# Banks of PSUM for the later bias units and for the small products, in a kernel of attention with a learned distance bias and a gated layer

## The chip, the cores and the metric

The kernel runs on one core of a Trainium2 chip. The metric is the time of one execution on the device, in microseconds (us), as the median of the runs; lower is better.

## The reference

Four sequences of 576 positions with 8 heads of width 64 go through attention with an additive bias, and the result, 2304 tokens of width 512, through a gated layer of width 1536:

```
rel  = pos[:, None] - pos[None, :]
x    = log1p(|rel|) / log1p(max(pos[:, None], 1))
bias = relu(x * w1 + b1) @ w2                    # (576, 576, 8 heads), hidden width 32
attn = softmax(q @ k.T / 8 + bias)               # per sequence and head
x    = (attn @ v), heads side by side            # 2304 x 512
out  = ((x @ w_a) * (x @ w_b)) @ w_out           # 512 -> 1536 -> 512
```

All inputs and the output are 32-bit floats; the large weights reach the kernel as 64-bit floats.

## The kernel before, in words

**Attention.** Two heads (a pair) of one sequence are a unit. The first half of the schedule takes query positions 0 to 255 of all units, the second half the other 320. A unit is cut into tiles of 128 queries against all 576 keys, 144 tiles in all. One tile is a chain over the engines: TensorE makes the scores in a pair of PSUM banks (`qk`, L444, or L458 for the first units), VectorE adds the bias row block and takes the minimum (L472), ScalarE takes the exponential (L477), GpSimd and VectorE form the reciprocal sum (L505, L506), GpSimd multiplies (L508), TensorE transposes (`tp`, L521), ScalarE and VectorE copy out (L526; L538 to L540), and after the last tile of a unit (of a pair of tiles, for the first four units) TensorE multiplies by the values (`pv`, L555, or L488). ScalarE and VectorE copy that out into the layer's input `x` (L495 and L496; L567 and L569). `attn_steps` issues this as two steps per tile, with loads some tiles ahead.

**The layer.** A block of 256 tokens takes 12 chunks `f` of the width 1536; for each, 12 products of `x` with w_a and then 12 with w_b go into one PSUM bank (`ab`, L649), ScalarE and VectorE copy out and multiply (L657, L659, which gives `g`), and after the chunks two outputs `o` of 36 products each follow (L698). Of the tag `ab`, which `o` shares, there are three banks.

**Weights.** `wab_steps` and `wo_steps` turn the 64-bit weights into 32-bit ones (`wt`, ScalarE L244, VectorE L245 to L249, from the load `wraw`, L238) and split them. A scale that is a power of two is found per pair of chunks by two small products: `pow2_down` (L62) transposes a column of maxima so that VectorE can reduce it (L66 to L72), and `pow2_up` (L75) spreads the result over the partitions (L77, L79). The same two serve the scale of the values of each sequence (`v_scale`). There are 10 of each in the program. Both put their product, `pr`, into the one PSUM bank of `pv`.

**The bias.** It depends on the positions alone and is made once, in 36 units of 16 query positions for all heads (`bias_unit`, L138): four hidden groups `h` (VectorE L126 or ScalarE L130), four products of each into PSUM (`psta`, L136), two scaled copies by ScalarE (`bo`, L151 and L154: one for each direction of the distance), and a store to DRAM, from where tiles load their rows (L424). Units over 512 columns are cut in two at column 288. The first 16 units come before attention. The 20 later ones (`bias_stream`, L806) are spread over tiles of the second and third sequence: `attn_steps` makes one, at times two, after the scores of a tile were read and before the next scores are issued. Their `psta` takes the pair of banks of the scores.

**PSUM.** Of the 8 banks `qk` has two, `tp` two, `pv` one, and the pools `eq` (two banks, at first) and `mps` (the three of `ab`, later) share the other three, of which one is unused while `eq` is open.

**Order.** TensorE's order is the program's own, fixed by `merge`, which interleaves the generators by their step counts. The other engines' queues are ordered by a scheduler when the kernel is built. Every engine's queue runs in order, as does that of SyncE (SP), which issues the loads.

```
ps = pvp.tile([128, 512], F32, tag="pv", name="pr")             # L63, L76
ab = mps.tile([128, 2, TOK], F32, tag="ab", name="ab", bufs=3)   # L644
pss = banks()                                                    # L145, one pair for both cuts
bg, lambda: qkp.tile([128, 2, 512], F32, tag="qk", name="psta", bufs=1), u, un, int(un % 4 != 3), 1, 2   # L809
```

Of the kernel before, what the change touches and what calls it, by code (L numbers as in the profile page):

```python
# [7 lines left out]
F32 = mybir.dt.float32  # L8
# [17 lines left out]
TOK = 256  # L26
# [21 lines left out]
def attention_moe(ctx, tc, q0d, q1d, kd, vd, idn, wp, wa, wb, wo, lsw, lg, rl, out):  # L48
    nc = tc.nc
    PSUM = bass.MemoryType.PSUM  # L50
# [8 lines left out]
    xt, cpool, epool, xpool = [], [None], [None], [None]  # L59
    vsc = []  # L60

    def pow2_down(mx, n, tag):  # L62
        ps = pvp.tile([128, 512], F32, tag="pv", name="pr")  # L63
        nc.tensor.matmul(ps[0:n, 0:128], mx, tab["idn"], start=True, stop=True)
        m = att.tile([n, 1], F32, tag="p2m" + tag, name="p2m", bufs=2)
        nc.vector.reduce_max(out=m, in_=ps[0:n, 0:128], axis=AX.X)  # L66
        nc.vector.tensor_scalar(out=m, in0=m, scalar1=3.0e38, scalar2=2.0 ** -100, op0=ALU.min, op1=ALU.max)
        nc.vector.tensor_scalar(
            out=m.bitcast(I32), in0=m.bitcast(I32), scalar1=0x7F800000, scalar2=None, op0=ALU.bitwise_and
        )  # L70
        dg = att.tile([n, n], F32, tag="p2d" + tag, name="p2d", bufs=2)
        nc.vector.tensor_scalar(out=dg, in0=tab["idn"][0:n, 0:n], scalar1=m, scalar2=None, op0=ALU.mult)  # L72
        return dg

    def pow2_up(dg, n, tag):  # L75
        ps = pvp.tile([128, 512], F32, tag="pv", name="pr")  # L76
        nc.tensor.matmul(ps[:, 0:n], tab["one"][0:n, :], dg, start=True, stop=True)  # L77
        g = att.tile([128, n], F32, tag="p2g" + tag, name="p2g", bufs=2)
        nc.vector.tensor_copy(g, ps[:, 0:n])  # L79
        return g  # L80
# [57 lines left out]
    def bias_unit(bg, banks, u, un, nact, hbufs, bufs):  # L138
        n = bias_span(un)
        hs = bias_relu(bg, u, un, nact, hbufs)  # L140
        ob = bg.tile([128, BW], F32, tag="bo", name="bo", bufs=bufs)
        mid, right = 16 * un + 15, S - 16 * un
        rl = tab["rl"][:, un:un + 1]
        cuts = [0, n] if n <= 512 else [0, HB, n]
        pss = banks()  # L145
        for x, (c0, c1) in enumerate(zip(cuts, cuts[1:])):
            ps = pss[:, x, :]
            bias_mm(ps[:, :c1 - c0], hs, c0, c1)
            e = min(c1, right)
            if e > c0:  # L150
                nc.scalar.mul(ob[:, mid + c0:mid + e], ps[:, :e - c0], rl)  # L151
            a, e = max(c0, 1), min(c1, mid + 1)
            if e > a:
                nc.scalar.mul(ob[:, mid + 1 - e:mid + 1 - a], ps[:, a - c0:e - c0][:, ::-1], rl)  # L154
        rows = bias_d[:, un, :].rearrange("h (r w) -> r h w", w=BW)
        nc.scalar.dma_start(out=rows[:, :, :BW - 1], in_=ob[:, :BW - 1])
        yield
# [600 lines left out]
    wtmp = wstack.enter_context(tc.tile_pool(name="wtmp", bufs=1))  # L758
    wab, won = wab_steps(wtmp), wo_steps(wtmp)
    wtp[1] = wtmp  # L760
    with tc.tile_pool(name="bg", bufs=1, side="right") as bg, tc.tile_pool(name="eq", bufs=1, space=PSUM) as eq:
        epool[:] = bg, eq
        bias_tables()
        tab["idn"] = cst.tile([128, 128], F32, name="idn")
# [29 lines left out]
        merge((asteps, 2), (fl, NP))  # L794
        merge((asteps, 8), (v_scale(0), 7), (wab, 3))
        merge((asteps, 2 * ends[0] - 10), (wab, 10))
    wop = ctx.enter_context(tc.tile_pool(name="wop", bufs=1, side="right", reuse_waits="tile"))
    mps = ctx.enter_context(tc.tile_pool(name="mps", bufs=1, space=PSUM, reuse_waits="tile"))
    for f in range(FC):
# [6 lines left out]
    def bias_stream(bg, u):  # L806
        for un in range(NU0, NU):
            yield from bias_unit(
                bg, lambda: qkp.tile([128, 2, 512], F32, tag="qk", name="psta", bufs=1), u, un, int(un % 4 != 3), 1, 2  # L809
            )  # L810

    nb = NU - NU0
# [76 lines left out]
```

## Time and profile before

| | |
|---|---|
| median of 3 runs | 875.76 us (875.16 to 878.99) |
| the profiled execution | 875.48 us, its span 873.4 us |
| busy: TensorE products, VectorE, ScalarE, GpSimd | 780.3, 546.0, 512.5, 308.4 us |
| loads and stores | 114.16 MB, 131 GB/s in the mean |

The span runs from the first to the last instruction; the 2.1 us between it and the execution's own time lie around it. Busy times are sums over the whole span, and the stretches differ: which engine sets the time is read stretch by stretch. Times in rows count from the span's start. A matmul of 32-bit floats stands as two records, so `x8` is four of them.

### The profile page before, as it was taken

Reading aid. Unit: us, or ns where it says so; the run is one execution under the profiler, and the core shown is the slowest. Engines: PE = TensorE matmul, PEld = TensorE weight load, DVE = VectorE, ACT = ScalarE, POOL = GpSimd, SP = SyncE. Lnnn points to the kernel's source line nnn. Section 1 sums busy time; section 2 is a strip of 40 time slices with the busy share of each in tenths; the row PEclk is TensorE's granted clock in tenths of the full one; section 3 lists DMA queues with packets and bytes.
Section 4 is the critical chain, followed back from the end, with each engine's and each line's share of the span. In section 5 each row is a group of like instructions: output and inputs, shape, how many; then the busy total and the mean of one; then the engine's idle time right before and its main releaser. Section 6 shows DMA issues by size and latency. Waiting matters only on the chain.

```text
span 873.4 us, 16482 instructions
## 1 busy us (share of the span) xinstructions
PE 780.3 (89%) x5936; PEld 622.9 (71%) x5936; DVE 546.0 (63%) x1291; ACT 512.5 (59%) x1102; POOL 308.4 (35%) x480
## 2 busy tenths in 40 slices
PE   5865669878888698988999999999999999999998
PEld 1244446647777466765888888888898898888886
DVE  5545577879799667765587778777787665210100
ACT  4747557857686467764577667766776666331310
POOL 0022446747366412321244433432443344220210
PEclk9959688969998799999999999999999999999999
DMA  7897265724776345443444444444443432100001
GB/s 214 242 298 237 77 217 185 208 60 126 232 231 186 91 141 163 139 120 100 127 126 130 130 139 147 118 133 137 117 121 125 127 87 65 55 2 25 1 10 39
DMA packets 52596, 114.16 MB, mean 131 GB/s; under 512 B 5156, under 2 KB 9508, under 8 KB 52516
## 3 DMA queue, kind: packets, MB, share of 16 engines
q1 hardware_dynamic: 44336, 97.34, 36.9%
q10 hardware_dynamic: 8180, 15.77, 6.1%
q8 instruction: 47, 0.77, 0.4%
q14 instruction: 33, 0.27, 0.1%
HBM read 95.91 MB, written 17.18 MB: 129 GB/s over the span
## 4 chain that ended last, share of the span: by engine, by line
PE 66%; DVE 11%; DMA 10%; ACT 6%; issue 4%; SPq 1%; POOL 1%; ACTq 0%; DVEq 0%; POOLq 0%
PE ab L649 25%; PE o L698 17%; PE tp L521 8%; PE qk L444 8%; PE pv L555 5%; PE psta L136 3%; DMA rv<-vd 2%; DMA wraw<-wb 2%; DVE p L472 2%; DMA bias<-bias_d 2%; ACT p L477 1%; DVE ks L373 1%; DVE wt L246 1%; DVE wt L249 1%; DMA rvf<-vd 1%
## 5 line engine op out<-in xcount | busy, mean ns | idle before, releaser
L649 PEld LDWEIGHTS <-w16t 128*128 128x128 f16 x2592 | 254.1, 99 | 44.2 <-issue 12.7
L649 PE MATMUL ab<-x,w16t 128*128 128x256 f16 x2304 | 276.5, 277 | 0.0
L472 DVE CUSTOM_DVE_ANT_0 p<-qk,bias 128x576 f32<-128x576 f32 x144 | 108.7, 755 | 90.4 <-PE tp L521 80.1
L508 POOL TENSOR_SCALAR p<-p,rc 128x576 f32<-128x576 f32 x144 | 126.5, 879 | 70.9 <-DVE rc L506 64.2
L538 ACT CAST pt<-tp 128x640 f16<-128x640 f32 x128 | 88.3, 690 | 101.9 <-PE tp L521 101.4
L477 ACT ACTIVATE p<-p,mn 128x576 f32<-128x576 f32 x144 | 111.7, 776 | 47.6 <-DVE mn L472 45.3
L521 PE MATMUL tp<-idn,p 128*128 128x128 f32 x720 | 111.7, 289 | 20.3 <-DVE pt L540 8.1
L505 POOL TENSOR_SCALAR rr<-sm 128x1 f32<-128x1 f32 x144 | 31.2, 217 | 278.0 <-ACT p L477 274.8
L698 PE MATMUL o<-wos,gh 128*128 128x512 f32 x384 | 124.4, 405 | 0.0
L674 POOL TENSOR_TENSOR gl<-g,gh 128x256 fp32r<-128x256 f32 x96 | 72.6, 758 | 132.0 <-ACT gh L673 130.8
L521 PEld LDWEIGHTS tp<-idn,p 128*128 128x128 f32 x720 | 87.8, 148 | 39.0 <-issue 19.9
L539 DVE TENSOR_TENSOR pt<-tp,pt 128x512 f16<-128x512 f32 x128 | 88.0, 688 | 8.6 <-ACT pt L538 8.3
L659 DVE SCALAR_TENSOR_TENSOR g<-ab,wv,asb 128x256 f32<-128x256 f32 x84 | 40.3, 482 | 82.2 <-ACT asb L657 80.9
L698 PEld LDWEIGHTS o<-wos,gh 128*128 128x128 f32 x384 | 69.1, 190 | 17.8 <-issue 5.4
L444 PE MATMUL qk<-ks,qs 128*128 128x288 f32 x384 | 73.2, 313 | 4.9 <-DVE mn L472 3.8
L698 PE MATMUL o<-wos,gl 128*128 128x512 f32 x192 | 75.8, 395 | 0.0
L136 PE MATMUL psta<-h,w2s 128*32 128x288 f32 (+17 forms) x352 | 48.7, 558 | 25.4 <-ACT bo L154 12.2
L444 PEld LDWEIGHTS qk<-ks,qs 128*128 128x128 f32 x384 | 57.3, 192 | 10.5 <-DVE mn L472 5.3
L657 ACT ACTIVATE asb<-ab,wv 128x256 f32<-128x256 f32 x84 | 39.2, 468 | 40.4 <-PE ab L649 40.3
L673 ACT CAST gh<-g 128x256 fp32r<-128x256 f32 x96 | 38.7, 405 | 35.1 <-DVE g L659 34.8
L555 PE MATMUL pv<-pt,vs 128*64 128x320 f16 (+1 forms) x784 | 56.5, 298 | 0.0
L126 DVE TENSOR_SCALAR h<-u,lgs 128x576 f32<-128x576 f32 (+17 forms) x117 | 46.4, 456 | 14.9 <-PE psta L136 14.5
(92 smaller groups left out, 977.0 us busy)
## 6 DMA issues: line engine op xcount, KB each, us to landing
bias<-bias_d SPq DMA_DIRECT2D x128, 288.0 KB
rv<-vd SPq DMA_DIRECT2D x40, 320.0 KB
bias_d<-bo ACTq DMA_DIRECT2D x36, 295.5 KB
rk<-kd SPq DMA_DIRECT2D x24, 288.0 KB
wraw<-wa SPq DMA_DIRECT2D x12, 512.0 KB
wraw<-wb SPq DMA_DIRECT2D x12, 512.0 KB
wraw<-wo SPq DMA_DIRECT2D x12, 512.0 KB
rq<-q1d SPq DMA_DIRECT2D x16, 320.0 KB
```

Of the source, the lines that this page charges most:

```text
L136: nc.tensor.matmul(dst[32 * g:32 * g + 32], tab["w2"], hs[g][:, c0:c1], start=True, stop=True)
L444: nc.tensor.matmul(ps[:, hf, :HB], a, b[:, hf * HB:hf * HB + HB], start=(x == 0), stop=(x == len(prods) - 1))
L472: ttr = nc.vector.tensor_tensor_reduce(out=p.rearrange("p (a n) -> p a n", a=2), in0=ps[:, :, :HB], in1=bt.rearrange("p (a n) -> p a n", a=2),
L477: exps.append(nc.scalar.activation(p, p, AF.Exp, bias=mn, scale=-1.0, accum_out=sm))
L508: nc.gpsimd.tensor_scalar(out=p, in0=p, scalar1=rc, scalar2=1.0, op0=ALU.mult, op1=ALU.mult)
L521: nc.tensor.transpose(tp[:, x, :], p[:, c0:c0 + 128], tab["idn"])
L538: nc.scalar.copy(dst[:, 0:5], src)
L539: nc.vector.tensor_tensor(out=dst[:, 5:9], in0=src[:, 0:4], in1=dst[:, 0:4], op=ALU.subtract)
L555: nc.tensor.matmul(ps[64 * j:64 * j + 64, :N], vs[:, part, vb, j, :], pt[:, pb, j * N:j * N + N], start=(x == 0), stop=(x == len(TERMS) - 1),)
L649: nc.tensor.matmul(ab[:, j], w16[nm, f][:, pw, kk, :], xs[px][:, kk, :], start=(x % (3 * KC) == 0), stop=(x % (3 * KC) == 3 * KC - 1),)
L674: nc.gpsimd.tensor_tensor(out=gl, in0=g, in1=gh.bitcast(F32), op=ALU.subtract)
L698: nc.tensor.matmul(o, g[:, sl], wos[f][:, p], start=(f == 0 and x == 0), stop=(f == FC - 1 and x == 2))
```

## The change

It touches three things. `pow2_down` and `pow2_up` take their product's place from `pr_tile`: while the pool `eq` is open, a pool `prp` with one bank of its own (the one that was unused); after that one of the three banks of `ab`. The later bias units take banks of `ab` in place of the scores' pair. And a unit that is cut in two asks for a new place when the first is used up: the first 16 units still get a pair from the scores' pools, the later ones a single bank for each cut, so 24 banks for 20 units (of these, the last four are over 512 columns).

```diff
@@ -59,8 +59,16 @@
     xt, cpool, epool, xpool = [], [None], [None], [None]
     vsc = []
 
+    prp = [None]
+
+    def pr_tile():
+        if prp[0]:
+            return prp[0].tile([128, 512], F32, tag="pr", name="pr", bufs=1)
+        return mps.tile([128, 2 * TOK], F32, tag="ab", name="pr", bufs=3)
+
+
     def pow2_down(mx, n, tag):
-        ps = pvp.tile([128, 512], F32, tag="pv", name="pr")
+        ps = pr_tile()
         nc.tensor.matmul(ps[0:n, 0:128], mx, tab["idn"], start=True, stop=True)
         m = att.tile([n, 1], F32, tag="p2m" + tag, name="p2m", bufs=2)
         nc.vector.reduce_max(out=m, in_=ps[0:n, 0:128], axis=AX.X)
@@ -73,7 +81,7 @@
         return dg
 
     def pow2_up(dg, n, tag):
-        ps = pvp.tile([128, 512], F32, tag="pv", name="pr")
+        ps = pr_tile()
         nc.tensor.matmul(ps[:, 0:n], tab["one"][0:n, :], dg, start=True, stop=True)
         g = att.tile([128, n], F32, tag="p2g" + tag, name="p2g", bufs=2)
         nc.vector.tensor_copy(g, ps[:, 0:n])
@@ -142,9 +150,11 @@
         mid, right = 16 * un + 15, S - 16 * un
         rl = tab["rl"][:, un:un + 1]
         cuts = [0, n] if n <= 512 else [0, HB, n]
-        pss = banks()
+        pss = None
         for x, (c0, c1) in enumerate(zip(cuts, cuts[1:])):
-            ps = pss[:, x, :]
+            if pss is None or x == pss.shape[1]:
+                pss, x0 = banks(), x
+            ps = pss[:, x - x0, :]
             bias_mm(ps[:, :c1 - c0], hs, c0, c1)
             e = min(c1, right)
             if e > c0:
@@ -758,7 +768,8 @@
     wtmp = wstack.enter_context(tc.tile_pool(name="wtmp", bufs=1))
     wab, won = wab_steps(wtmp), wo_steps(wtmp)
     wtp[1] = wtmp
-    with tc.tile_pool(name="bg", bufs=1, side="right") as bg, tc.tile_pool(name="eq", bufs=1, space=PSUM) as eq:
+    with tc.tile_pool(name="bg", bufs=1, side="right") as bg, tc.tile_pool(name="eq", bufs=1, space=PSUM) as eq, \
+            tc.tile_pool(name="prp", bufs=1, space=PSUM) as prp[0]:
         epool[:] = bg, eq
         bias_tables()
         tab["idn"] = cst.tile([128, 128], F32, name="idn")
@@ -794,6 +805,7 @@
         merge((asteps, 2), (fl, NP))
         merge((asteps, 8), (v_scale(0), 7), (wab, 3))
         merge((asteps, 2 * ends[0] - 10), (wab, 10))
+    prp[0] = None
     wop = ctx.enter_context(tc.tile_pool(name="wop", bufs=1, side="right", reuse_waits="tile"))
     mps = ctx.enter_context(tc.tile_pool(name="mps", bufs=1, space=PSUM, reuse_waits="tile"))
     for f in range(FC):
@@ -806,7 +818,7 @@
     def bias_stream(bg, u):
         for un in range(NU0, NU):
             yield from bias_unit(
-                bg, lambda: qkp.tile([128, 2, 512], F32, tag="qk", name="psta", bufs=1), u, un, int(un % 4 != 3), 1, 2
+                bg, lambda: mps.tile([128, 1, 2 * TOK], F32, tag="ab", name="psta", bufs=3), u, un, int(un % 4 != 3), 1, 2
             )
 
     nb = NU - NU0
```

TensorE makes the same products in the same order. What changes there is what they wait for; on VectorE, ScalarE, GpSimd and SP the scheduler also puts some instructions elsewhere, mostly between the weights' conversion and the first two sequences' attention. Lines of the changed kernel stand 8 higher in the first functions, 10 higher from `bias_unit` on.

First place: TensorE at the eighth of the 20 small products (`pr`), at 130 us of the trace before. (`waits` names the engine or load queue whose semaphore an instruction waits for, with the program's suffix.) Before:

```order
L521 MATMUL tp<-idn,p 128x128 x4
L488 MATMUL pv<-ptf,rvf 64x128 x10
L77 MATMUL pr<-p2d,one 128x4 [waits DVE_49]
L444 MATMUL qk<-rkf,rqf 128x288 [waits DMAHW7_49]
L444 MATMUL qk<-rkf,rqf 128x288
L521 MATMUL tp<-idn,p 128x128 [waits Activation_49,Pool_49]
```

and now:

```order
L531 MATMUL tp<-idn,p 128x128 x4
L498 MATMUL pv<-ptf,rvf 64x128 [waits DVE_49]
L498 MATMUL pv<-ptf,rvf 64x128 x9
L85 MATMUL pr<-p2d,one 128x4
L454 MATMUL qk<-rkf,rqf 128x288 [waits DMAHW7_49,DVE_49]
L454 MATMUL qk<-rkf,rqf 128x288
L531 MATMUL tp<-idn,p 128x128 [waits DVE_49,Activation_49,Pool_49]
```

The small product no longer waits; the scores behind it now carry the wait for VectorE's read of the last scores, which they need in any case.

Second place: VectorE around the 13th and 14th small product (`p2m` and `p2d` are the small tiles of `pow2_down`), at 175 to 182 us of the trace before. Before:

```order
L245 TENSOR_SCALAR wt<-wt 128x512
L246 SCALAR_TENSOR_TENSOR wt<-wraw,wt 128x512
L506 RECIPROCAL rc<-rr 128x1
L249 SCALAR_TENSOR_TENSOR wt<-wraw,wt 128x512
L245 TENSOR_SCALAR wt<-wt 128x512
L569 SCALAR_TENSOR_TENSOR x_1480<-pv,x_1479 128x256
L246 SCALAR_TENSOR_TENSOR wt<-wraw,wt 128x512
L408 SCALAR_TENSOR_TENSOR vs<-rv,vs_938,vs 128x640
L245 TENSOR_SCALAR wt<-wt 128x512
L66 TENSOR_REDUCE p2m<-pr 4x1
L249 SCALAR_TENSOR_TENSOR wt<-wraw,wt 128x512
```

and now:

```order
L74 TENSOR_REDUCE p2m<-pr 4x1
L74 TENSOR_REDUCE p2m<-pr 1x1
L75 TENSOR_SCALAR p2m<-p2m 4x1
L75 TENSOR_SCALAR p2m<-p2m 1x1
L76 TENSOR_SCALAR p2m<-p2m 4x1
L76 TENSOR_SCALAR p2m<-p2m 1x1
L80 TENSOR_SCALAR p2d<-idn,p2m 4x4
L80 TENSOR_SCALAR p2d<-idn,p2m 1x1
L255 TENSOR_SCALAR wt<-wt 128x512
L579 SCALAR_TENSOR_TENSOR x_1484<-pv,x_1483 128x256
L256 SCALAR_TENSOR_TENSOR wt<-wraw,wt 128x512
L516 RECIPROCAL rc<-rr 128x1
```

The reductions of the two small products (L66, now L74) and what follows them have moved ahead of a group of weight conversions (L245 to L249, now L255 to L259) and of the copy of the values' product (L569, now L579).

Third place: TensorE at the second cut of a late bias unit (`h` are the hidden groups, `w2s` the second weights; 256 columns are the second cut), at 391 to 395 us of the trace before. Before:

```order
L136 MATMUL psta<-h_4678,w2s 32x288
L136 MATMUL psta<-h_4680,w2s 32x288 [waits Activation_49]
L136 MATMUL psta<-h_4674,w2s 32x256 [waits Activation_49]
L136 MATMUL psta<-h_4676,w2s 32x256
L136 MATMUL psta<-h_4678,w2s 32x256
L136 MATMUL psta<-h_4680,w2s 32x256
L649 LDWEIGHTS w16t
L649 MATMUL ab<-x_2676,w16t 128x256
```

and now:

```order
L144 MATMUL psta<-h_4683,w2s 32x288 [waits DVE_49]
L144 MATMUL psta<-h_4685,w2s 32x288 [waits Activation_49]
L144 MATMUL psta<-h_4679,w2s 32x256 [waits PE_49]
L144 MATMUL psta<-h_4681,w2s 32x256
L144 MATMUL psta<-h_4683,w2s 32x256
L144 MATMUL psta<-h_4685,w2s 32x256
L659 LDWEIGHTS w16t [waits PE_49]
L659 MATMUL ab<-x_2680,w16t 128x256 [waits Activation_49]
```

The second cut waited for ScalarE; now it waits for an earlier product of TensorE's own alone, and the layer's product behind it waits for ScalarE instead.

## Rows read from the trace of the kernel before

**Rows 1.** Stretches of the span: its limits in us from the span's start and its length, then busy time and number of instructions of TensorE's products (PE), its weight loads (PEld), VectorE (DVE), ScalarE (ACT) and GpSimd (POOL), the granted clock, the DMA share and GB/s.

```profile
55.00:140.00 85.00, 55.94 (x351) 39.46 (x351) 50.87 (x139) 51.71 (x117) 32.34 (x49) 0.76 0.59 195
...
173.00:189.00 16.00, 8.77 (x43) 5.11 (x38) 12.03 (x32) 8.20 (x19) 6.17 (x6) 0.63 0.20 55
189.00:293.00 104.00, 90.53 (x747) 74.48 (x747) 93.25 (x205) 74.84 (x154) 63.95 (x76) 0.93 0.58 175
301.00:408.00 107.00, 95.88 (x763) 67.06 (x762) 73.00 (x170) 70.11 (x148) 25.98 (x43) 0.96 0.46 132
...
500.00:873.00 373.00, 369.02 (x2872) 320.67 (x2871) 190.11 (x440) 188.73 (x404) 116.80 (x200) 1.00 0.28 85
```

**Rows 2.** TensorE's instructions in order of time, 85 to 135 us: start, us from the start of the first to the end of the last, engine, line, operation, tiles, form, count, and in brackets the idle time just before and what ended it.

```profile
88.48 0.58 PE L64 MATMUL pr<-idn,vm 128*1 128x128 f32 x2 [4.76 <-DVE x L496]
...
93.73 1.31 PE L488 MATMUL pv<-ptf,rvf 128*64 128x128 f32 x20
98.61 0.58 PE L77 MATMUL pr<-p2d,one 1*128 1x1 f32 x2 [3.56 <-DVE x L496]
...
112.02 0.48 PE L64 MATMUL pr<-idn,wm 128*4 128x128 f32 x2 [1.70 <-DVE x L496]
...
123.38 1.31 PE L488 MATMUL pv<-ptf,rvf 128*64 128x128 f32 x20
130.26 0.58 PE L77 MATMUL pr<-p2d,one 4*128 4x4 f32 x2 [5.57 <-DVE x L496]
```

**Rows 3.** VectorE's in the same stretch, with the same columns.

```profile
84.89 0.16 DVE L208 TENSOR_REDUCE vm<-vmx 128x1 f32<-128x4 f32 x1 [0.72 <-ACT rv L200]
...
89.76 0.20 DVE L72 TENSOR_SCALAR p2d<-idn,p2m 1x1 f32<-1x1 f32 x1
92.23 0.76 DVE L472 CUSTOM_DVE_ANT_0 p<-qk,bias 128x576 f32<-128x576 f32 x1 [2.27 <-PE tp L521]
...
103.67 0.76 DVE L472 CUSTOM_DVE_ANT_0 p<-qk,bias 128x576 f32<-128x576 f32 x1 [2.99 <-PE tp L521]
...
125.04 0.75 DVE L472 CUSTOM_DVE_ANT_0 p<-qk,bias 128x576 f32<-128x576 f32 x1
...
134.36 0.76 DVE L472 CUSTOM_DVE_ANT_0 p<-qk,bias 128x576 f32<-128x576 f32 x1 [2.99 <-PE tp L521]
```

**Rows 4.** The chain of waits that ended last, 139 to 170 us: start, us, what.

```profile
139.89 4.71 DMA rv<-vd
...
146.58 6.56 DMA wraw<-wb
...
153.20 7.57 DMA wraw<-wb
...
161.42 6.62 DMA wraw<-wb
```

**Rows 5.** TensorE's instructions in order of time, 171 to 185 us.

```profile
171.84 1.72 PE L555 MATMUL pv<-pt,vs 128*64 128x256 f16 x28
179.45 0.59 PE L64 MATMUL pr<-idn,wm 128*4 128x128 f32 x2 [5.89 <-DVE x L569]
181.90 2.74 PE L649 MATMUL ab<-x,w16t 128*128 128x256 f16 x12
```

**Rows 6.** VectorE's in order of time, 173 to 192 us.

```profile
173.61 0.15 DVE L208 TENSOR_REDUCE vm<-vmx 128x1 f32<-128x4 f32 x1
...
185.19 0.48 DVE L659 SCALAR_TENSOR_TENSOR g<-ab,winv,asb 128x256 f32<-128x256 f32 x1 [1.19 <-ACT asb L657]
188.16 0.76 DVE L472 CUSTOM_DVE_ANT_0 p<-qk,bias 128x576 f32<-128x576 f32 x1 [2.48 <-PE tp L521]
...
191.05 0.16 DVE L79 COPY p2g<-pr 128x4 f32<-128x4 f32 x1 [1.17 <-PE pr L77]
```

**Rows 7.** ScalarE's in order of time at 173 us.

```profile
173.30 0.63 ACT L266 ACTIVATE w16t<-wt 128x512 f16<-128x512 f32 x1
```

**Rows 8.** TensorE's in the stretch of the later bias units, 301 to 408 us.

```profile
340.96 0.79 PE L444 MATMUL qk<-ks,qs 128*128 128x288 f32 x4 [1.05 <-ACT bo L154]
...
345.64 1.41 PE L136 MATMUL psta<-h,w2s 128*32 128x416 f32 x8 [1.10 <-ACT bo L154]
...
371.91 1.61 PE L136 MATMUL psta<-h,w2s 128*32 128x496 f32 x8 [1.10 <-ACT bo L154]
...
386.65 0.61 PE L136 MATMUL psta<-h,w2s 128*32 128x240 f32 x8 [0.85 <-ACT bo L154]
387.20 1.49 PE L649 MATMUL ab<-x,w16t 128*128 128x256 f16 x12
...
391.00 0.69 PE L136 MATMUL psta<-h,w2s 128*32 128x288 f32 x8
394.63 0.64 PE L136 MATMUL psta<-h,w2s 128*32 128x256 f32 x8 [2.94 <-ACT bo L154]
395.20 2.50 PE L649 MATMUL ab<-x,w16t 128*128 128x256 f16 x12
...
402.14 0.67 PE L136 MATMUL psta<-h,w2s 128*32 128x272 f32 x8 [0.82 <-ACT bo L154]
...
406.48 0.69 PE L136 MATMUL psta<-h,w2s 128*32 128x288 f32 x8 [0.76 <-ACT bo L154]
```

**Rows 9.** The chain that ended last, at 394 us: start, us, what.

```profile
394.18 0.40 ACT bo L154
```

## The prediction

> **What bounds the kernel now.** I read the table of stretches first [rows 1]. From 500 us to the end TensorE is busy 369.0 of 373 us at the full granted clock: whatever is won before that point arrives at the end in full, and nothing can be won after it. Before 408 us no engine is full. Three stretches matter. From 55 to 140 us TensorE works 55.9 of 85 us, VectorE 50.9, the DMA engines 0.59: that is a chain of waits, not a load. From 173 to 189 us everything stalls: TensorE 8.8 of 16 us, ScalarE 8.2, GpSimd 6.2, DMA share 0.20. From 189 to 293 us VectorE works 93.3 of 104 us and is the bound. From 301 to 408 us TensorE works 95.9 of 107 us with VectorE at 73.0, so TensorE sets the pace and its gaps are paid.
>
> Next, TensorE in order of time, to see what ends its gaps. In the first stretch four small products wait for VectorE's copy of the values' product (L496), 4.76, 3.56, 1.70 and 5.57 us [rows 2]. They have no use for that copy: they wait because their product goes into the one bank that it is still reading. In the second, the small product at 179.45 waits for the same kind of copy (L569) and the layer's product behind it starts at 181.90, though TensorE was done with its last work at 171.84 + 1.72 = 173.56 [rows 5]. In the stretch of the bias units TensorE waits seven times for ScalarE's scaled copies (L154), 8.6 us in all [rows 8]: the second cut, the second unit of a step, or the scores behind a unit want the same pair of banks.
>
> Last, VectorE, to see what such a wait costs others. Behind the waits it runs dry: 2.27, 2.99 and 2.99 us before scores that TensorE delivered late [rows 3], and 1.19, 2.48 and 1.17 us after the stall at 173 us [rows 6].
>
> **The change, part by part.** No operation is added or taken away, and TensorE's order stays. So only waits change, and I go by place.
>
> *Small products, 55 to 140 us.* With a bank of their own they wait for their operand alone. At 88.48 that is the maximum at 84.89 + 0.16 = 85.05 [rows 3]: 3.4 us earlier. At 98.61 the operand was there at 89.96, before TensorE ended the values' product at 95.04 [rows 2, 3]: all 3.6 us go. At 112.02, 1.7 us go. At 130.26 TensorE was free at 124.69, but the scores behind must wait until VectorE has read the last ones at 125.04 + 0.75 = 125.79 [rows 2, 3]: 4.5 us of 5.6. Together 13.2 us on TensorE's clock. How much reaches the end is unknown: the weights' loads and conversions have to keep up. The bounds are nothing (the chain runs through loads from 140 on [rows 4]) and 13.2. I take the time that VectorE, the bound of what follows, stood idle for TensorE behind these waits: 2.27 + 2.99 + 2.99 = **8.25 us**.
>
> *Small products, 173 to 189 us.* The first one's operand is ready when ScalarE ends the row sum at 173.9, the second one's at 173.76 [rows 6, 7]; TensorE would reach the layer's product at about 174.6 instead of 181.90: 7.3 us, the upper bound. But VectorE converted weights meanwhile, work that it must still do. By the same measure as above I take its idle time, 1.19 + 2.48 + 1.17 = **4.84 us**; the lower bound is nothing. That the reductions now stand ahead of the conversions helps here: in the old order they would have kept TensorE's next products waiting. What is late next is the conversion, which VectorE then has to do in the stretch from 189 us on, where it is the bound.
>
> *Small products from then on* take one of the three banks of the layer. None of them is on a wait in these rows, and the banks' old contents are read about as early as before: nothing.
>
> *Later bias units.* Scores no longer wait for the copies: 1.05 us at 340.96. The second unit of a step, 1.10 us at 345.64 and at 371.91, must still wait for its hidden groups, since these have one buffer that the unit before was using: half, 1.1 us for both. Second cuts: 0.85, 0.82 and 0.76 us at 386.65, 402.14 and 406.48. The wait of 2.94 us at 394.63 mostly stays: the layer's product behind the unit now needs the bank of the first cut, whose copy ends at the same 394.58 [rows 9], so only the second cut's own 0.64 us moves into the gap. Sum 1.05 + 1.1 + 2.43 + 0.64 = **5.2 us**. The upper bound is all 8.6 us and, since the layer's product after the longest wait took 2.50 us where 1.49 is usual [rows 8], another 1.0 us. The lower bound is negative and is a rival below.
>
> The new tenants shorten the ring of three: a bank must now be copied out one product sooner. Between the end of a layer's product, 387.20 + 1.49 = 388.69, and the next bias unit at 391.00 there are 2.3 us of other work [rows 8], and a copy that ends later than that stops TensorE. From 500 us on, the same three banks rotate with only products and outputs of the layer in them, at a granted clock of 1.00 [rows 1]. The Trainium skill speaks against such rotation: "TensorE: Matmul & The Clock Gate", section "A second HAM failure mode: psum-queue depth-cycling", tells of a kernel that cycled through banks in each iteration, idled briefly between groups and had its clock fall and rise. This trace does not agree for the ring as it stands; with every product beside the 24 banks at the rate seen at 395.20, by that rule the sum would be 24 us worse.
>
> *Sum.* 8.25 + 4.84 + 5.2 = 18.3 us. The profiled execution took 875.48 us, so **857.2 us**. It lies 0.28 us under the median of the runs shown, so the two scales are one.
>
> **The rivals.**
>
> *The front gives nothing back.* From 140 to 168 us the chain is four loads, 4.71, 6.56, 7.57 and 6.62 us [rows 4], and VectorE is full after 189. If loads and conversions set the time up to 293 us, the first two terms are zero and only the bias units count: 875.48 − 5.2 = 870.3 us. For it: the same weights must come in and be converted. Against it: DMA shares of 0.59 and 0.20, and idle time of all engines in the very gaps.
>
> *The waits only move.* The product at 394.63 shows how: the wait leaves the bias unit and stands before the next product. If it is so everywhere, and the front gives nothing, the time stays, about 875 us.
>
> *The ring of three becomes the wait; slower.* Place: the later bias units. Each time that a copy ends after TensorE wants its bank, it costs what the row at 394.63 shows: 2.94 us, and 2.50 − 1.49 = 1.0 us for the product behind at the lower clock level, 3.95 us together. The point is a copy more than 2.3 us behind its product; there the copy ended 394.58 − 391.69 = 2.9 us behind. Six such stops eat the gain and 4.4 us more; at a third of the 24 banks, eight stops, it is 857.2 + 31.6 = 889 us. The page named above would have it so. Against it: of the seven waits in the rows, one alone exceeds 1.1 us.
>
> **How the numbers follow.** A measurement can tell a change of about 0.5%, 4.4 us, from none. Forecast 857 us: 0.52. Front gives nothing: 0.22. Waits only move: 0.14. Ring: 0.12. The first two are faster by over 0.5%, so 0.74 faster, 0.14 the same, 0.12 slower. The range begins at the upper bounds of all terms, 875.48 − 13.2 − 7.3 − 9.6 = 845 us, and ends at 873 us, past the first rival and short of the last two; with a part of the second in it, it leaves out about 2 in 10.
>
> **What would show it.** Right: no small product waits for L496 or L569; VectorE's idle time before scores shrinks by some 8 us up to 140 us; the layer's product now at 181.90 starts within 2 us of the values' product before it, and the scores' reading now at 188.16 follows some 5 us sooner relative to it; in the bias stretch waits of scores for L154 are gone. TensorE's last gaps of the bias stretch end some 18 us earlier than now. The prediction is wrong if the stretch up to 293 us ends where it did, with VectorE idle for loads instead of for TensorE, or if layer's products and bias units wait for L154 or L659 by more than 5 us in all.

## The result, and the profile after

The changed kernel takes 852.19 us (median of 4 runs, 850.46 to 853.46) beside 875.46 us for the kernel before on the same chip: a ratio of 0.9727, 95% interval 0.9706 to 0.9748. Forecast were 857.2 us. The profiled execution took 852.24 us, its span 850.1 us. Run a second time beside other kernels it took 851.66 us, ratio 0.9715 (0.9687 to 0.9744).

The stretches of the changed kernel, by the same limits and with the same columns as [rows 1] (the last ends earlier, since the span does):

```profile
55.00:140.00 85.00, 61.84 (x435) 44.37 (x435) 62.45 (x170) 59.65 (x137) 44.16 (x57) 0.83 0.71 228
...
173.00:189.00 16.00, 10.04 (x60) 6.46 (x60) 13.27 (x29) 9.24 (x20) 11.47 (x13) 0.79 0.33 88
189.00:293.00 104.00, 84.23 (x714) 70.27 (x709) 86.83 (x194) 71.33 (x147) 57.08 (x68) 0.93 0.57 173
...
301.00:408.00 107.00, 98.35 (x832) 73.25 (x831) 76.42 (x172) 69.47 (x148) 27.70 (x48) 1.00 0.47 136
...
500.00:850.00 350.00, 346.12 (x2726) 301.33 (x2726) 173.62 (x402) 174.44 (x377) 109.90 (x186) 1.00 0.28 82
```

From 55 to 140 us 435 records of products fit where 351 did, and the granted clock rose from 0.76 to 0.83. But equal times no longer hold equal work. TensorE's order is the same in both kernels, so its products mark stretches of equal work. First the kernel before, from the transposes at 79.1 us to the layer's product at 135.6, from there to the transposes at 171.6, to the layer's product at 189.2, to the first late bias unit at 300.7, and to a second cut at 402.1:

```profile
79.11:135.61 56.50, 36.22 (x213) 24.94 (x211) 34.23 (x92) 32.25 (x73) 23.53 (x34) 0.76 0.54 178
135.61:171.64 36.03, 31.77 (x225) 23.46 (x223) 31.81 (x75) 28.29 (x67) 24.39 (x29) 0.95 0.69 201
171.64:189.19 17.55, 10.31 (x62) 6.43 (x61) 13.55 (x33) 9.75 (x23) 6.99 (x8) 0.65 0.19 54
189.19:300.71 111.52, 92.74 (x763) 75.94 (x762) 97.19 (x215) 77.51 (x160) 67.86 (x80) 0.93 0.57 172
300.71:402.14 101.43, 92.11 (x735) 65.67 (x735) 70.71 (x166) 68.14 (x144) 24.84 (x42) 0.95 0.47 134
```

The same work in the changed kernel:

```profile
80.63:120.01 39.38, 29.72 (x212) 20.76 (x212) 29.80 (x85) 29.37 (x70) 22.93 (x30) 0.87 0.64 205
120.01:158.75 38.74, 31.94 (x226) 23.50 (x223) 34.24 (x81) 28.97 (x67) 28.84 (x33) 0.95 0.79 239
158.75:167.29 8.54, 7.84 (x62) 5.54 (x61) 6.94 (x23) 8.54 (x20) 6.62 (x7) 0.81 0.33 90
167.29:283.17 115.88, 90.15 (x764) 74.33 (x761) 101.50 (x225) 79.83 (x165) 71.47 (x82) 0.93 0.55 166
283.17:379.91 96.74, 89.60 (x736) 65.14 (x740) 71.11 (x163) 66.64 (x142) 23.60 (x40) 0.97 0.48 138
```

Length less busy time is TensorE's idle time. In the first stretch it fell from 56.50 − 36.22 = 20.3 to 39.38 − 29.72 = 9.7 us, 10.6 less. The *same* 212 records of products also took 6.5 us less, at a granted clock of 0.87 for 0.76. That second part is in no term of the prediction. Over the whole span TensorE's busy time fell from 780.3 to 767.8 us, 12.5 of the 23.2 us that the profiled executions differ by.

The waits went as the diff says. TensorE in the changed kernel, at the four products of [rows 2]:

```profile
86.74 0.44 PE L72 MATMUL pr<-idn,vm 128*1 128x128 f32 x2 [2.22 <-DVE vm L218]
...
93.36 0.38 PE L85 MATMUL pr<-p2d,one 1*128 1x1 f32 x2
...
101.85 0.38 PE L72 MATMUL pr<-idn,wm 128*4 128x128 f32 x2
...
116.31 0.38 PE L85 MATMUL pr<-p2d,one 4*128 4x4 f32 x2
```

Three wait for nothing, the first waits for its operand alone; no small product waits for the copies of L496 or L569 (now L506, L579) any more. Three take 0.38 us, at a granted clock of 1.00 while they run, the upper of the clock's two levels (2.4 GHz); in [rows 2] three took 0.58 us, at 0.50, the lower (1.2 GHz). And at the stall of [rows 5]:

```profile
159.09 3.13 PE L565 MATMUL pv<-pt,vs 128*64 128x256 f16 x28
162.92 0.38 PE L72 MATMUL pr<-idn,wm 128*4 128x128 f32 x2 [0.70 <-ACT w16t L276]
163.14 0.38 PE L72 MATMUL pr<-idn,vm 128*1 128x128 f32 x2
163.45 1.48 PE L659 MATMUL ab<-x,w16t 128*128 128x256 f16 x12
...
181.34 0.59 PE L72 MATMUL pr<-idn,wm 128*4 128x128 f32 x2 [3.98 <-ACT w16t L276]
181.86 4.76 PE L659 MATMUL ab<-x,w16t 128*128 128x256 f16 x24
```

The layer's product starts 163.45 − 162.22 = 1.2 us after the values' product has ended, not 8.3. At 181 us the wait for scaled weights has grown to 3.98 us. The same product in the kernel before:

```profile
199.09 0.38 PE L64 MATMUL pr<-idn,wm 128*4 128x128 f32 x2 [1.11 <-ACT w16t L266]
```

For what follows, the **lead** is the start of the same product of TensorE in the profile of before less its start in this one, both counted from the first product (us; the heads are times of the kernel before):

| kernel | 79 | 136 | 172 | 189 | 301 | 407 | end |
|---|---|---|---|---|---|---|---|
| changed | −1.6 | 15.5 | 12.8 | 21.8 | 17.5 | 22.5 | 23.0 |
| changed, second time | −0.8 | 19.0 | 15.7 | 24.6 | 18.9 | 23.4 | 23.9 |
| small products only | −0.8 | 15.2 | 16.4 | 25.6 | 20.8 | 21.7 | 21.6 |
| bias units only | −2.5 | −3.0 | −3.1 | −3.1 | −4.0 | 0.9 | 1.5 |
| first small products only | −2.1 | 13.9 | 12.7 | 13.6 | 14.5 | 14.4 | 15.0 |
| later small products only | −1.5 | 0.4 | −0.9 | 10.5 | 4.4 | 4.3 | 5.0 |
| before, waits filled | −1.4 | 6.7 | 5.8 | 9.7 | 9.8 | 10.3 | 10.8 |
| VectorE's reads held back | −0.5 | 13.4 | 6.8 | 16.8 | 11.8 | 15.8 | 16.1 |
| bias units in `pv`'s bank | −0.5 | 12.6 | 13.4 | 19.6 | 14.9 | 16.2 | 16.3 |
| changed, waits filled | −0.1 | 16.2 | 13.1 | 22.7 | 18.3 | 24.3 | 24.6 |
| less conversion | −2.5 | 7.4 | 4.9 | 15.7 | 15.0 | 19.5 | 19.9 |
| conversions held behind | 3.8 | 14.6 | 11.9 | 23.2 | 16.5 | 20.5 | 20.9 |

Each row is one profiled execution, and not always a typical one: for "bias units only" the lead at the end is 1.5 us, while the median of its 8 runs is 6.2 us below that of the kernel before. So a time is taken from the medians, and a place from the leads and waits.

### The profile page after: what moved, and what is told of

Read it like the earlier page. It is cut to its first block, busy times and chain, and to the rows that moved or that the text cites. A ratio compares the mean times of both kernels' runs of the same rounds, so it can differ in the third digit from the quotient of the medians.

```text
span 850.1 us, 16457 instructions
## 1 busy us (share of the span) xinstructions
PE 767.8 (90%) x5936; PEld 616.4 (73%) x5936; DVE 543.4 (64%) x1291; ACT 511.0 (60%) x1102; POOL 314.7 (37%) x480
## 4 chain that ended last, share of the span: by engine, by line
PE 65%; DVE 12%; DMA 10%; ACT 5%; issue 4%; SPq 1%; POOL 1%; ACTq 0%; DVEq 0%; POOLq 0%
PE ab L659 25%; PE o L708 18%; PE tp L531 7%; PE qk L454 7%; PE pv L565 5%; DMA rv<-vd 3%; PE psta L144 3%; DMA bias<-bias_d 2%; DVE p L482 2%; DVE wt L259 2%; DVE wt L256 1%; ACT p L487 1%; DVE ks L383 1%; DMA rvf<-vd 1%; DVE pt L549 1%
## 5 line engine op out<-in xcount | busy, mean ns | idle before, releaser
L659 PEld LDWEIGHTS <-w16t 128*128 128x128 f16 x2592 | 251.7, 98 | 45.5 <-issue 16.1
L659 PE MATMUL ab<-x,w16t 128*128 128x256 f16 x2304 | 271.4, 274 | 3.7 <-ACT bo L164 2.5
L531 PE MATMUL tp<-idn,p 128*128 128x128 f32 x720 | 107.6, 282 | 22.4 <-DVE pt L550 8.7
L531 PEld LDWEIGHTS tp<-idn,p 128*128 128x128 f32 x720 | 84.6, 143 | 40.0 <-issue 19.7
L669 DVE SCALAR_TENSOR_TENSOR g<-ab,wv,asb 128x256 f32<-128x256 f32 x84 | 40.3, 482 | 81.5 <-ACT asb L667 80.5
L134 DVE TENSOR_SCALAR h<-u,lgs 128x576 f32<-128x576 f32 (+17 forms) x117 | 48.4, 472 | 12.8 <-PE psta L144 12.5
```

Of the source, the lines that this page charges most:

```text
L531: nc.tensor.transpose(tp[:, x, :], p[:, c0:c0 + 128], tab["idn"])
L659: nc.tensor.matmul(ab[:, j], w16[nm, f][:, pw, kk, :], xs[px][:, kk, :], start=(x % (3 * KC) == 0), stop=(x % (3 * KC) == 3 * KC - 1),)
```

## The experiments

**The parts by themselves.** The theory was that each term stands by itself, the rivals that VectorE or the loads swallow a part alone.

*Small products only* (the late units' banks put back):

```diff
-bg, lambda: mps.tile([128, 1, 2 * TOK], F32, tag="ab", name="psta", bufs=3), u, un, ...
+bg, lambda: qkp.tile([128, 2, 512], F32, tag="qk", name="psta", bufs=1), u, un, ...
```

> Only the small products move (own bank, later one of the three of the layer); the later bias units keep the scores' pair. Theory A, the terms stand by themselves: the trace of the changed kernel is 17.5 us ahead of the one before when the bias units begin at 283 us and 22.2 us ahead when they end, so without the bias part some 18 us of the 23 are left, about 857.5 us (855 to 860). Rival B, the terms depend on each other (VectorE from 189 us on swallows what the front wins unless the bias units give it room): 865 us or more.

859.54 us, ratio 0.9823 (0.9779 to 0.9867). Its four runs spread from 853.8 to 865.8, so the median says little more than that most of the gain is here. The trace, of the fastest of the four, shows the place: 20.8 us of lead at 301, and with the old pair only 0.9 more over the bias units, where the changed kernel wins 5.0.

*Bias units only* (both places of `pr_tile` are again `pvp.tile([128, 512], F32, tag="pv", name="pr")`):

> Only the later bias units move; all small products stay in the bank of the values' product. Theory A: the lead grows by 4.7 us over the bias stretch, so about 870.8 us (869 to 872.5). Rival C, the waits only move (the layer's product behind the unit waits in place of the scores): within 1.5 us of the kernel before, 875 us. Rival D, the ring of three costs more than it gives: over 877 us.

870.17 us, ratio 0.9933 (0.9906 to 0.9959). The lead grows by 4.9 us from 301 to 407, with nothing won ahead of it: the term stands by itself, and "the waits only move" and "the ring costs more" are both out.

*First small products only* (own bank at first, later `pv`'s; bias units as before):

> Only the small products up to 140 us of the kernel before get a bank of their own; later ones and the bias units as before. Theory A: the changed kernel's lead was 12.0 us at 172 us of the kernel before, after 15 us at 136: about 863.5 us (861 to 866). Rival E, the loads of the weights from 140 on set the time, the lead at 172 us is there only since the later products wait less too: 869 us or more.

861.99 us, ratio 0.9826 (0.9794 to 0.9857). The lead of 12.7 us at 172 is kept to the end.

*Later small products only* (`pv`'s bank at first, later the layer's; bias units as before):

> Only the small products from 140 us on move to the layer's three banks; the first ones and the bias units as before. Theory A: the stall at 173 to 189 us goes, 7 to 10 us at once, and VectorE's conversions take part of it back: 5 us, about 870.5 us (868.5 to 872). Rival F, the conversions take all of it back, since VectorE is full from 189 us on: 875 us.

869.62 us, ratio 0.9913 (0.9889 to 0.9937). Of 11.3 us won from 172 to 189, 6.1 are lost again by 301. Theory A held four times, in the medians within 2.1 us. The first small products, the later ones and the bias units alone gave 14.4, 6.7 and 6.2 us by the medians, 27.3 together, where the whole change gave 23.3 and 25.1 us: the difference is within the intervals.

**Idle time or clock?** The kernel before, with idle products (nobody reads their result) put into TensorE's five waits of 81 to 130 us; the waits stay:

```diff
+    FILL = {2: 3, 3: 10, 4: 7, 6: 3, 7: 12}
...
+    def fillers():
+        for _ in range(FILL.get(calls[0], 0)):
+            nc.tensor.matmul(fill[0][:, 0:128], tab["idn"], tab["idn"], start=True, stop=True)
+        calls[0] += 1
...
     def pow2_down(mx, n, tag):
+        fillers()
         ps = pvp.tile([128, 512], F32, tag="pv", name="pr")
```

(the same ahead of the product of `pow2_up`; `FILL` goes by the number of the small product, `fill` is the unused bank, and `...` stands for lines left out, here and below)

> The kernel before, with 35 idle products of the identity by itself put into TensorE's five waits of 81 to 130 us (3, 10, 7, 3 and 12 of them, written to the unused bank, read by nobody); the waits themselves stay. Between 79 and 136 us of the kernel before, the same 212 products took 36.2 us there and 29.7 us in the changed kernel, at a granted clock of 0.76 and 0.87. Theory K, a part of the first term is the clock that came back when the gaps went: with the gaps full the products behind them run faster, the lead over the kernel before is 3 to 6 us at 136 us, and the time 870 to 873 us. Rival L, the idle time is all of it: the time stays at 876 us, or grows by what the fillers delay.

864.67 us, ratio 0.9856 (0.9831 to 0.9881): 12 us, with no wait taken away. TensorE's order of time around three of the fillings:

```profile
85.07 2.50 PE L67 MATMUL fill<-idn 128*128 128x128 f32 x20
90.58 0.38 PE L73 MATMUL pr<-idn,vm 128*1 128x128 f32 x2 [3.01 <-DVE x L506]
...
95.61 1.83 PE L67 MATMUL fill<-idn 128*128 128x128 f32 x14
98.76 0.38 PE L87 MATMUL pr<-p2d,one 1*128 1x1 f32 x2 [1.32 <-DVE x L506]
...
122.44 2.94 PE L67 MATMUL fill<-idn 128*128 128x128 f32 x24
126.00 0.38 PE L87 MATMUL pr<-p2d,one 4*128 4x4 f32 x2 [0.61 <-DVE x L506]
```

and the stretch of equal work (79 to 136 us of the kernel before), first all of it, then the fillers alone (columns: length, TensorE's products, weight loads, VectorE, ScalarE, GpSimd, granted clock, DMA share, GB/s; the second row has the first two engines only):

```profile
80.43:128.83 48.40, 36.33 (x281) 27.72 (x281) 31.62 (x90) 31.10 (x72) 20.90 (x32) 0.93 0.60 185
```

```profile
80.43:128.83 48.40, 8.94 (x70) 8.20 (x70) 0.93 0.60 185
```

The granted clock is 0.93 instead of 0.76. Idle time and fillers make 48.40 − 36.33 + 8.94 = 21.0 us, where the idle time was 20.3: nothing of the waits is gone. The real products take 36.33 − 8.94 = 27.4 us instead of 36.2, some 8.8 less (fillers and products overlap a little at their seams; the stretch is 8.1 shorter). So in this stretch products at the upper clock are worth about 8 us by themselves. The other 4 come from elsewhere: the scheduler moved some of VectorE's rows here too, the copy of the values' product at 172 to 189 us now stands ahead of a group of conversions, and TensorE's wait for it fell from 5.89 to 3.17 us. The lead grows by 3.9 us there.

**Is VectorE's order part of it?** The changed kernel with every reduction and copy of a small product held behind the last copy of a values' product (`xc` holds those copies):

```diff
+    def behind():
+        return tc.issue_after(xc[-1].ins) if xc else nullcontext()
...
-        nc.vector.reduce_max(out=m, in_=ps[0:n, 0:128], axis=AX.X)
+        with behind():
+            nc.vector.reduce_max(out=m, in_=ps[0:n, 0:128], axis=AX.X)
```

> The changed kernel, with VectorE's reads of the small products (the reduction and the copy) forced behind its last copy of a values' product, as the shared bank forced them before; the banks stay. Theory M, it was TensorE standing at the bank that cost: TensorE still goes on without a wait, and the time stays within 3 us of the changed kernel, 850 to 855 us. Rival N, it was VectorE's order that gained, the reductions being ahead of copies and conversions: the later product of the pair waits for its operand in place of the bank, and 5 us or more of the 23 are lost, 857 us and more.

859.79 us, ratio 0.9817 (0.9781 to 0.9853). Rival N has its part: some 8 us of the 23 need the order that the bank made possible. From 172 to 189 the lead grows by 10.0 us, as in the changed kernel. From 136 to 172 it loses 6.7, where the changed kernel lost 2.7 and 3.3: there TensorE waits for the operand in place of the bank, 4.86 us where the changed kernel waits 2.02. And from 79 to 136 it wins 14.0 us instead of 17.1 and 19.8, with 12.1 us of idle time instead of 9.7 and 8.8.

```profile
137.66 0.58 PE L90 MATMUL pr<-p2d,one 4*128 4x4 f32 x2 [4.86 <-DVE p2d L85]
```

The edit holds the reads behind the copies, not behind the weights' conversions. VectorE in this run, at the 13th and 14th small product: the copy (L585), both reductions (L79), and a group of conversions (from L261) after them.

```profile
169.50 0.42 DVE L585 SCALAR_TENSOR_TENSOR x<-pv,x 128x256 f16<-128x256 f32 x1 [1.17 <-ACT x L583]
169.84 0.47 DVE L79 TENSOR_REDUCE p2m<-pr 4x1 f32<-4x128 f32 x2
...
171.29 1.52 DVE L261 TENSOR_SCALAR wt<-wt 128x512 int32<-128x512 int32 x2
```

**What takes back 4 to 6 us from 189 to 301?** The changed kernel without the last conversion step of the last four weight blocks of w_a and w_b (where the new argument is false, the step is left out, and those weights lose their sign):

```diff
-            wfs[s] = wab_conv(*raws.pop(s))
+            wfs[s] = wab_conv(*raws.pop(s), s < 20)
```

> The changed kernel without VectorE's last step (the sign) in the conversion of the last four weight blocks of the first two matrices, four operations of some 0.68 us; their values lose the sign. In the changed kernel VectorE has no gap from 163 to 185 us of its trace, and TensorE waits 3.98 us at 181 us for the scaled weights; from 189 to 301 us of the kernel before the lead falls from 21.8 to 17.5 us. Theory V, VectorE's conversions take that back: with 2.7 us less of them the wait at 181 us falls by 2 us or more, the lead at 301 us grows by 2 to 3 us, about 849.5 us. Rival W, loads or ScalarE take it back: VectorE runs idle instead, and the time stays at 852 us.

850.62 us, ratio 0.9701 (0.9652 to 0.9749): not clear of the changed kernel's 851.7 and 852.2. In the profile the wait at 181 us is gone:

```profile
184.47 0.38 PE L72 MATMUL pr<-idn,wm 128*4 128x128 f32 x2
```

From 189 to 301 the lead falls by 0.7 us instead of 4.4 and 5.7. In the first profile of the changed kernel three waits at 174 to 181 us make 4.8 us more than before; here those three are gone, and two others make 2.3 us more than before. A smaller lead does not explain it: the later small products alone lost 6.1 us from a lead of 10.5, the held-back reads 5.0 from 16.8. So theory V holds for the mechanism: VectorE's conversions are what is late next. What their time is worth at the end is not shown, because this execution was behind already at 136. Its first two rows of equal work (79 to 136 and 136 to 172), then the one from 189 to 301:

```profile
81.63:128.22 46.59, 38.24 (x212) 26.53 (x211) 32.45 (x90) 31.70 (x73) 25.40 (x33) 0.67 0.64 204
128.22:166.68 38.46, 34.30 (x225) 24.51 (x223) 33.24 (x80) 29.45 (x69) 26.46 (x29) 0.87 0.70 211
...
173.45:285.70 112.25, 91.98 (x764) 75.87 (x761) 98.91 (x224) 79.37 (x165) 68.27 (x81) 0.94 0.57 172
```

Idle time in the first is 8.4 us, as little as in the changed kernel, but the products take 38.2 us at a granted clock of 0.67, and the edit's place lies behind them.

**One bank or several for the bias units?** The changed kernel with `psta` from `pvp.tile([128, 1, 512], F32, tag="pv", name="psta")`:

> The changed kernel, but the later bias units take the single bank of the values' product in place of the layer's three. Theory P, what the third term pays for is that scores no longer share a place with the units: any other bank does, 851 to 853.5 us, as the changed kernel. Rival Q, it needs the several banks: with one, a second cut waits for the copies of the first again, as with the scores' pair, and the lead over the bias stretch falls from 4.7 to 1 us or so, 856 us or more.

856.12 us, ratio 0.9779 (0.974 to 0.9817). Rival Q holds: the lead grows by 1.3 us over the bias units instead of 5.0, and the second cuts of [rows 8] wait as they did:

```profile
370.54 0.61 PE L144 MATMUL psta<-h,w2s 128*32 128x240 f32 x8 [0.90 <-ACT bo L164]
...
378.51 0.72 PE L144 MATMUL psta<-h,w2s 128*32 128x256 f32 x8 [2.94 <-ACT bo L164]
```

**Does the same filling help the changed kernel?** Idle products in five of its remaining waits, four ahead of small products and one, of 28 products, ahead of the first late bias unit, written to the bank that the next product overwrites:

```diff
+    FILL = {1: 12, 3: 5, 9: 7, 16: 14}
...
+            if un == NU0 and not x:
+                for _ in range(28):
+                    nc.tensor.matmul(ps[:, 0:128], tab["idn"], tab["idn"], start=True, stop=True)
```

> The changed kernel, with idle products of the identity in five of its remaining waits: 12, 5, 7 and 14 ahead of small products (at 55, 84, 131 and 177 us of its trace) and 28 ahead of the first later bias unit (waiting 7.1 us at 276 us), written to the bank that the product behind them overwrites. Theory K: the products behind keep the upper clock; 24 of the layer's took 4.76 us behind the wait at 181 us where 2.9 is usual, the unit at 283 us 1.87 for 0.9, the first stretch about 1.5: 4 us less than the changed kernel, 848 us (846 to 850). Rival L: nothing is won, 852 us, or some us are lost where fillers run past the wait.

852.58 us, ratio 0.9726 (0.9693 to 0.9759); the changed kernel beside it took 851.66. Nothing is won. The row of equal work from 189 to 301:

```profile
166.47:282.41 115.94, 99.54 (x848) 84.26 (x845) 103.29 (x227) 79.73 (x165) 71.01 (x81) 0.96 0.55 166
```

It is as long as without fillers (115.88), and in sum the program's own products are no faster: the two fillings took 3.29 and 6.41 us, the rest 89.8, where it was 90.15. At one place they did run faster, the layer's 24 products behind the wait at 181 us; at another they ran slower:

```profile
181.88 2.79 PE L672 MATMUL ab<-x,w16t 128*128 128x256 f16 x24
...
271.99 2.65 PE L578 MATMUL pv<-pt,vs 128*64 128x256 f16 x28
...
276.06 6.41 PE L170 MATMUL psta<-idn 128*128 128x128 f32 x56
```

Without fillers these were 4.76 and 1.72 us. The last wait, which the 28 fill, ends with the hidden groups, for which VectorE itself waits 2.96 us for a load here (3.44 in the changed kernel). So the run shows no gain from fillers here, and leaves open what a faster TensorE would be worth in this stretch.

**The changed kernel again**, on the chip of the two fillings and of the held-back reads:

> The changed kernel once more, beside the others on the same chip: 852 us (850 to 855), and how much of the lead at 136, 172, 189 and 301 us comes again in a second profile: within 2 us at each, if it is the change's and not the loads' luck.

851.66 us. The lead differs by 3.5 us at 136, by 2.9 at 172 and 2.8 at 189, more than expected, and by 1.4 at 301. In its first stretch the products took 27.89 us (29.72 the first time).

The other profiles say more. From 79 to 136 us three of them are of the kernel's order before and six of the changed order: there every engine does the same work in the same order within each group, and TensorE in all nine.

| kernel, its stretch from 79 to 136 | length | idle | products | granted clock |
|---|---|---|---|---|
| before | 56.5 | 20.3 | 36.2 | 0.76 |
| later small products only | 54.6 | 17.8 | 36.7 | 0.72 |
| bias units only | 57.0 | 17.2 | 39.7 | 0.68 |
| changed, second time | 36.7 | 8.8 | 27.9 | 0.91 |
| changed | 39.4 | 9.7 | 29.7 | 0.87 |
| first small products only | 40.5 | 9.1 | 31.4 | 0.83 |
| small products only | 40.6 | 9.2 | 31.4 | 0.83 |
| bias units in `pv`'s bank | 43.4 | 9.3 | 34.1 | 0.76 |
| less conversion | 46.6 | 8.4 | 38.2 | 0.67 |

The idle time follows the order: it differs by 1.3 us among the six, by 3.1 among the three. The products' time does not: it differs by 10.3 us among the six, and with it the lead at 136 goes from 7.4 to 19.0. In the mean of the two groups the stretch is 14.8 us shorter, 9.4 of idle time and 5.4 of products.

**An earlier wait.** The changed kernel's longest wait in the front, 5.59 us at 55 us, is for a reduction that VectorE has queued behind a conversion whose load is late. Here the conversions are held behind it:

```diff
+        with tc.issue_after(p2d[0].ins):
             nc.vector.tensor_scalar(out=t, in0=t, scalar1=3, scalar2=None, op0=ALU.logical_shift_left)
...
-        merge((asteps, 8), (v_scale(0), 7), (wab, 3))
-        merge((asteps, 2 * ends[0] - 10), (wab, 10))
+        next(wab)
+        merge((asteps, 8), (v_scale(0), 7))
+        merge((asteps, 2 * ends[0] - 10), (wab, 12))
```

> The changed kernel with VectorE's weight conversions forced behind the reduction of the first small product (in the changed kernel the first conversion stands ahead of it and waits 3.88 us for a load at 53 us, TensorE 5.59 us for the reduction's result at 55 us); the steps of the first weights are spread a little later for it, so that some small products stand elsewhere between the tiles. If waits and clock early in the program arrive at the end as the first term did: the wait falls to under 1.5 us, 4 us less at 61 us, and 847 to 849.5 us in the end. If the loads and conversions from 120 us on take it back: 852 us. If the conversions then come late for the layer's first products: above 853 us.

851.86 us, ratio 0.9726 (0.9689 to 0.9764): no gain. The wait fell as foreseen, and others came behind it:

```profile
55.92 0.58 PE L85 MATMUL pr<-p2d,one 1*128 1x1 f32 x2 [1.12 <-DVE p2d L80]
...
73.29 2.27 PE L469 MATMUL qk<-rkf,rqf 64*128 64x288 f32 x6 [2.23 <-DVE mn L483]
...
80.70 1.30 PE L532 MATMUL tp<-idn,p 128*128 128x128 f32 x5 [3.88 <-ACT ptf L537]
```

By VectorE's readings of the scores it is 5.8 us ahead of the first profile of the changed kernel at the 10th tile and 2.9 behind at the 25th. So time won before 75 us does not arrive by this way. It is lost in the stretch from 79 to 136:

```profile
75.49:121.19 45.70, 33.52 (x212) 23.97 (x211) 32.83 (x92) 33.18 (x77) 24.74 (x32) 0.76 0.71 217
```

Its idle time is 12.2 us where the changed kernel had 9.7, and the products took 33.5 us where they took 29.7 (granted clock 0.76, not 0.87). Whether loads or the later steps of the conversions make the waits was not told apart. No version here beats the changed kernel by more than the spread.

## Why the prediction was right, and where it was not

**The place and the direction** were right in all three terms. The sum, 18.3 us, was 5 short, and nearly all of that is one term.

| term | predicted | lead of the changed kernel | second profile | alone |
|---|---|---|---|---|
| small products to 140 us | 8.25 (0 to 13.2) | 12.8 at 172 | 15.7 | 12.7 |
| small products, 173 to 189 us | 4.84 (0 to 7.3) | +4.7 by 301 | +3.2 | +5.2 |
| later bias units | 5.2 (up to 9.6) | +5.0 by 407 | +4.5 | +4.9 |
| small products after that | 0 | +0.6 by the end | +0.6 | |

**First term: mis-sized.** The step was "I take the time that VectorE ... stood idle for TensorE", 8.25 us, with 13.2 as the upper bound. Both count only idle time. TensorE's did fall by 10.6 us, between the two; VectorE's waits for the transposes' end ahead of the scores fell from 9.2 to 3.0 us on the equal work, where I had expected 8 less. What failed is that each wait also cost the products behind it: 6.5 us at 136 in the first profile, 5.4 in the mean of the nine, and the filled waits show about 8 us for this part with the idle time left in. At 136 the lead was 17.1 us more than at 79, past my upper bound; 2.7 were lost again by 172, where waits for scaled weights (L276) made 2.3 us in place of 0.6. The granted clock of 0.76 in [rows 1] was the sign of this cost, and I gave it no price. By one profile the term's size is loose, since the lead at 172 goes from 4.9 to 16.4 us among the six of the changed order; the median of the first small products alone, 14.4 us, bears it out.

**Second term: right by size, a remark left open.** TensorE gained 9.0 us at once, more than the bound of 7.3, since here too the 62 records of products ran faster (10.31 to 7.84 us). Then 4.4 were lost again. "What is late next is the conversion, which VectorE then has to do in the stretch from 189 us on" is what the run with less conversion shows. That the reductions ahead of the conversions help here is not shown by any run: held back, they still stood ahead of the conversions from 172 to 189, and cost nothing there.

**Third term: right sum, wrong parts.** That 5.0 us came where 5.2 were forecast is in part luck. I had added up 5.2 us of waits. The idle time of equal work fell only from 9.3 to 7.1 us; the products gave the rest, 92.1 to 89.6 us. Of the two waits at the second unit of a step, of which I had counted half as gone, one grew from 1.10 to 2.55 us and the other stayed, at 1.05, now for hidden groups. The longest wait, which I had mostly let stand, did stand. TensorE in the changed kernel:

```profile
327.45 1.49 PE L144 MATMUL psta<-h,w2s 128*32 128x416 f32 x8 [2.55 <-DVE h L134]
...
371.98 1.12 PE L144 MATMUL psta<-h,w2s 128*32 128x288 f32 x16
375.61 1.47 PE L659 MATMUL ab<-x,w16t 128*128 128x256 f16 x12 [2.50 <-ACT bo L164]
```

The wait of 2.94 at the longest second cut moved to the layer's product as 2.50. That product then took 1.47 us at a granted clock of 1.00, not the 2.50 of [rows 8], at 0.56; now both cuts stand ahead of the wait and none behind it. No run separates why the clock held there.

**The rivals.** "The front gives nothing back" is refuted by the first small products alone: 12.7 us at 172, 15.0 at the end. Its mechanism, conversions that take the gain back, is real from 189 to 301; what takes back a gain from before 75 us is open. "The waits only move" holds for one wait of the bias stretch. The ring of three did not become the wait: the changed kernel's waits for its copies in the bias stretch are 2.50 us for L164 and 0.5 us for L669, under the 5 us that I had set. With 24 more tenants in the ring the granted clock on the equal work from 301 to 402 us rose from 0.95 to 0.97. What the Trainium skill's "TensorE: Matmul & The Clock Gate", section "A second HAM failure mode: psum-queue depth-cycling", tells of cycling through banks, a clock that falls and rises between the groups of products, does not agree with this trace.

## What to carry to other kernels

A wait of TensorE has two prices, the idle time and the products behind it at the lower clock level; cut the trace into stretches of equal work and take both, busy time and idle time, before summing. A PSUM bank that two users share makes one wait for the other's reader, though it needs no data from it: look for a releaser that the waiting instruction does not read. And what a part wins arrives only as far as the next engine is not full: from 189 to 301 us VectorE's conversions took 4 to 6 us back, and idle products there won nothing.

## What the runs showed of the hardware that was not expected

Idle products alone, 35 of them in five waits, made the kernel before 12 us faster, over half as much as the change. Some 8 us of it came with the granted clock of the stretch, 0.93 where it was 0.76; the rest came where the edit had also moved VectorE's order, with a shorter wait.

And the granted clock is not settled by the program: the same 212 records of products, with 8.4 to 9.7 us of idle time among them and the same order on every engine, took from 27.9 to 38.2 us in six profiles, at granted clocks from 0.91 to 0.67. A wait of 2.3 us ahead of 272 us was followed by products at the full clock in the changed kernel (1.72 us for the values' product) and by slower ones in the one with filled waits (2.65 us). What sets it was not found. It explains a part of the spread between runs: with the small products alone the run of 865.8 us had a mean granted clock of 0.938, the one of 853.8 us 0.959; but a run of 859.5 us had 0.960.
